# First-batch loads over 128 and 96 partitions, masks by matmul, partial products kept in open PSUM banks

## The chip, the cores and the metric

The kernel runs on one core of a Trainium2 chip. The metric is the device time of one execution in microseconds (us). A core has five engines with a queue of their own: TensorE (PE; its weight loads are listed apart as PEld), VectorE (DVE), ScalarE (ACT), GpSimd (POOL) and SyncE (SP), which here issues every DMA. A difference of about 0.3% (1.6 us) is what a measurement of this kernel can tell from no change.

## What is computed

Banded attention over 8 batches, 8 heads, 576 positions and 64 features a head, and then a gated block on its output:

```python
scores = scale * np.matmul(q, k.transpose(0, 1, 3, 2))
mask_plain = (rel >= 0) & (rel < 32)                          # heads 0 to 3
mask_dil = (rel >= 0) & (rel < 128) & (rel % 4 == 0)          # heads 4 to 7
attn = softmax(np.where(mask, scores, -1e9))
x = (attn @ v), heads joined                                  # (8, 576, 512)
h = np.maximum(x @ w_in, 0.0)                                 # w_in: 512 x 1024
u, v = h[..., :512], h[..., 512:]
v_n = (v - mean(v)) / np.sqrt(var(v) + 1e-06)
v_s = np.einsum('ts,bsd->btd', w_spatial, v_n) + b_spatial[None, :, None]
out = (u * v_s) @ w_out                                       # w_out: 512 x 512
```

The two weights `w_in` and `w_out` come as float64.

## The kernel before

**Tiling.** A pair of heads fills 128 partitions. For a pair, `heads_in` loads the keys and the queries (both transposed) into one of 12 buffers `kqv`, and `values_in` loads the values into another: four DMAs of 64 partitions, each row cut into nine runs of 64 numbers (L451). `unit` takes three blocks of 64 queries of two pairs: 24 score products of 32 queries by 64 keys (L469) that go to two PSUM banks, the mask added by DVE on the way out (L489), the maximum (L491), exponentials on ACT (one by one with their sums, L497, or all at once, L506, with the sum on DVE, L508), the division on POOL (L512), three transposes (L517) and a copy (L520). `weighted` multiplies by the values (L545): 36 products a call, two calls for two pairs, each with 64 rows of keys, and four that stand in a row use four different quarters of the array. `evacuated` and `features_in` turn the result into a rounded part `xh` and a remainder `xl`, four times for the 512 features.

**Precision.** Every large product is three products of rounded halves (hi by hi, hi by lo, lo by hi). For the weights `weight` makes the halves from the two words of a float64: a scaling on ACT (L319), four instructions on DVE (L321, L323, L326, L329), the rounding on ACT (L356), and the remainder by three matmuls and a copy (L335 to L339), by DVE (L280, L350) or by POOL. `weight_in` loads a block of 128 rows as two DMAs of 64 partitions (L297), since the two heads of a pair that stand together in `x` do not stand together in `w_in`.

**The rest of a batch.** `v_tile` (L614, L628) makes the half `v` of the hidden layer and normalises it, `upper` (L690, batch 0 only) the half `u`, `gate` (L711 to L713) the product with `w_spatial`. From batch 1 on `u`, and in every batch the output, come from `piece`: a product of two by two blocks with seven products (named 11, 21, 1, 2, 3, 22, 4) in place of eight, each of six matmuls (L831), whose inputs are sums and differences that `differences` (POOL, L821) and `factor` (ACT, L794, and DVE, L280) make. Every product has a PSUM bank of its own; the first is copied out by ACT (L874), and seven additions on DVE (L872) per half `m` put the results together.

**Order.** `Timeline.run` writes the program: every function above is a strand that asks for an engine with a cost and for buffers by tag (`kqv`, `mm`, `bank`, ...), and the strand that could start first, with a rank added, is recorded next. The ranks come from tables in the code. So each engine has one fixed order, and an engine waits where its next instruction isn't ready. `warm` fills gaps that the planner sees on PE before its time 30 with matmuls of zeros (L895); their number is fixed in the program.

Of the kernel before, what the change touches and what calls it, by code (L numbers as in the profile page):

```python
# [22 lines left out]
NEG = -(2.0**100)  # L23

# [123 lines left out]
def tile_banded_attention_gated_moe(  # L148
# [46 lines left out]
    BIG = NB * D  # L195

# [4 lines left out]
    def bufs(tag, shape, n, pool=const):  # L201
        return [pool.tile(shape, F32, name=f"{tag}{i}") for i in range(n)]


    tl = Timeline(
        dict(
            bank=bufs("bank", [P, 512], 8, ps),
            mm=[None] * 4,
            s=[None] * 2,
# [8 lines left out]
            ur=bufs("ur", [P, HS], 10),  # L218
            fac=[],
# [10 lines left out]
    kinds = tl.bufs["raw"][0][:, : 2 * KW].bitcast(BF16).rearrange("p (n k) -> p n k", n=4)  # L230
# [11 lines left out]
    for r in range(QB, P, QB):  # L242
        nc.vector.tensor_copy(kinds[r : r + QB], top)
    nc.vector.tensor_copy(masks, kinds[:, 0:1].broadcast_to([P, US + NS, KW]))

# [5 lines left out]
    for (far, g), n in cut.items():  # L251
        r = slice(g % 2 * 2 * QB, g % 2 * 2 * QB + 2 * QB)
        nc.vector.tensor_copy(masks[r, US * far + g // 2], kinds[r, n])
# [4 lines left out]
    nc.vector.tensor_scalar_mul(minus, draft, -1.0)  # L258
    ident = plus.bitcast(F32)
    halfneg = const.tile([P, 1], F32, name="halfneg")  # L260
    nc.gpsimd.memset(halfneg, -0.5)


    wi = [const.tile([P, NC, DFF], F32R, name=f"wi{n}") for n in "hl"]
    wo = [const.tile([P, NC, DM], F32R, name=f"wo{n}") for n in "hl"]
# [20 lines left out]

    staged = {}

    def weight_in(key, src):

        yield "kqv"
        (staged[key],) = yield DMA, 1.95, 1.5
        dtype = src[0].dtype
        place = staged[key][1][:, : 512 if dtype == F32 else 1024]
        rows = P // len(src)
        for i, part in enumerate(src):
            nc.sync.dma_start(place[i * rows : i * rows + rows].bitcast(dtype), part)  # L297
        tl.done("in", *key)

    def weight(key, hi, lo, dtype, how):  # L300

        yield [("in", *key)]
# [56 lines left out]
    def spatial_in(sc):  # L359
        yield "kqv"  # L360
        (staged[sc],) = yield DMA, 1.1, 1.5
        nc.sync.dma_start(staged[sc][1][:, :S], w_spT[:, sc, :])
        tl.done("in", sc)

    def spatial(sc):
# [6 lines left out]
        if sc < 4:  # L372
            nc.scalar.copy(wt[0][:, sc, :], w)
            if not (sc in (1, 2,)):
                yield DVE2, 0.75
                sub(wt[1][:, sc, :], w, wt[0][:, sc, :])
            for ts in (slice(0, HS), slice(HS, S)) if sc in (1, 2,) else ():
# [45 lines left out]
    def heads_in(b, hp, lo=0, hi=NU):  # L423
# [5 lines left out]
        got = yield DMA, 0.74 * (hi - lo), 1.5  # L429
# [25 lines left out]
    def unit(b, G, u):  # L455
# [3 lines left out]
        yield [("qk", b, hp, u) for hp in pairs] + ([("v", 0, 1)] if b == 1 else [])  # L459
        yield "s bank bank p"  # L460
        *held, pb = yield PE, 0.52, 0.0
# [698 lines left out]
```

## Time and profile before

| | |
|---|---|
| median of 3 runs | 548.06 us (546.82 to 548.44) |
| the profiled execution, first to last instruction | 544.7 us |
| median less that span | 3.4 us |
| PE, DVE, ACT, POOL busy | 98%, 80%, 56%, 39% |
| matmuls recorded | 7591 |

The page gives no other time of the profiled execution than its span; the 3.4 us are what a run takes beyond the first and the last instruction, as far as these two numbers tell. A plain f32 matmul (L335, L469, L545) has two records and the matmuls of zeros (L895) one, so counts of records and of instructions differ: 1152 score products in the program have 2304 records. Durations of matmuls overlap; the distance from one start to the next is what a matmul costs PE.

### The profile page before, as it was taken

The page shows a single profiled execution, that of the slowest core. Times are in us where ns is not written, and L with a number is a line of the kernel's source. Part 1 is how long each engine was busy: PE and PEld are TensorE (multiplying, and loading weights), DVE is VectorE, ACT ScalarE, POOL GpSimd, SP SyncE. Part 2 cuts the span into 40 slices and gives each one's busy share as a digit, 9 for nine tenths or more (in the row PEclk, how much of TensorE's full clock was granted, in tenths as well). Part 3 has the DMA queues.
Part 4 walks back from the last instruction along what each step waited for, and adds up shares of the span by engine and source line. Part 5 has one row for each costly group of instructions (what it writes and reads, how often), then busy time and mean ns, then how long its engine had stood idle before and what let it go on. Part 6 is the DMA issues. An engine that isn't in the chain of part 4 may idle for free.

```text
span 544.7 us, 18357 instructions
## 1 busy us (share of the span) xinstructions
PE 536.1 (98%) x7591; PEld 487.9 (90%) x7591; DVE 435.7 (80%) x1036; ACT 307.1 (56%) x939; POOL 215.1 (39%) x255
## 2 busy tenths in 40 slices
PE   9998999999999999999999999999999999999997
PEld 7766789999998899988999999988999899989997
DVE  5988778989956998489957998489956899479836
ACT  4787796455755555565454555556464565454312
POOL 3420385373426153524417163433417153253230
PEclk9999999999999999999999999999999999999999
DMA  8999741201463144511464135421454134301002
GB/s 236 250 185 339 162 105 59 91 22 66 109 160 91 45 134 90 150 52 55 113 127 132 45 113 106 122 75 56 113 121 147 44 113 94 65 12 44 34 1 87
DMA packets 97446, 56.65 MB, mean 104 GB/s; under 512 B 78290, under 2 KB 87506, under 8 KB 97364
## 3 DMA queue, kind: packets, MB, share of 16 engines
q1 hardware_dynamic: 97364, 55.50, 38.4%
q8 instruction: 59, 0.97, 0.8%
q14 instruction: 23, 0.19, 0.1%
HBM read 46.04 MB, written 9.44 MB: 102 GB/s over the span
## 4 chain that ended last, share of the span: by engine, by line
PE 93%; DMA 3%; ACT 2%; issue 1%; SPq 1%; DVE 0%; POOL 0%
PE bank L831 31%; PE bank L711 19%; PE bank L614 16%; PE bank L545 6%; PE bank L469 5%; PE bank L517 3%; PE bank L628 2%; PE bank L690 2%; PE bank L895 2%; PE bank L713 2%; PE bank L712 2%; PE bank L335 1%; DMA kqv<-in_vw_dram 1%; DMA kqv<-in_w_in_dram 1%; ACT p L497 1%
## 5 line engine op out<-in xcount | busy, mean ns | idle before, releaser
L872 DVE TENSOR_TENSOR ur<-ur,bank 128x288 f32<-128x288 f32 x210 | 87.4, 446 | 28.3 <-PE bank L831 27.9
L794 ACT CAST fac<-ur 128x288 fp32r<-128x288 f32 x112 | 46.0, 430 | 79.8 <-DVE ur L718 40.3
L711 PE MATMUL bank<-wth,vnh 128*128 128x288 f32 x256 | 76.5, 299 | 0.0
L280 DVE TENSOR_TENSOR fac<-ur,fac 128x288 fp32r<-128x288 f32 x112 | 60.5, 550 | 19.5 <-ACT fac L794 19.2
L711 PE MATMUL bank<-wth,vnl 128*128 128x288 f32 x256 | 75.6, 295 | 0.1
L711 PE MATMUL bank<-wtl,vnh 128*128 128x288 f32 x256 | 75.6, 295 | 0.0
L821 POOL TENSOR_TENSOR ur<-ur,ur 128x288 f32<-128x288 f32 x64 | 55.5, 877 | 44.1 <-DVE ur L718 34.0
L512 POOL TENSOR_TENSOR p<-p,rv 128x384 f32<-128x384 f32 x48 | 40.8, 851 | 74.5 <-DVE rv L510 63.4
L497 ACT ACTIVATE p<-p,nm 128x64 f32<-128x64 f32 x192 | 64.5, 337 | 8.8 <-DVE nm L491 8.7
L650 POOL TENSOR_TENSOR rs<-rs,halfneg 128x1 f32<-128x1 f32 (+1 forms) x40 | 29.3, 732 | 91.1 <-DVE rs L648 91.0
L831 PE MATMUL bank<-fac,woh 128*128 128x288 f32 x256 | 53.3, 298 | 0.1
L614 PE MATMUL bank<-wih,xl 128*128 128x512 f32 x128 | 50.1, 392 | 1.8 <-issue 1.8
L821 POOL TENSOR_TENSOR raw<-raw,raw 128x288 f32<-128x288 f32 x42 | 43.3, 1037 | 19.4 <-DVE fac L280 18.6
L614 PE MATMUL bank<-wih,xh 128*128 128x512 f32 x128 | 50.4, 394 | 0.0
L614 PE MATMUL bank<-wil,xh 128*128 128x512 f32 x128 | 50.2, 392 | 0.0
L711 PEld LDWEIGHTS bank<-wth,vnh 128*128 128x128 f32 x256 | 48.2, 188 | 0.4
L711 PEld LDWEIGHTS bank<-wth,vnl 128*128 128x128 f32 x256 | 48.1, 188 | 0.3 <-issue 0.3
L711 PEld LDWEIGHTS bank<-wtl,vnh 128*128 128x128 f32 x256 | 48.2, 188 | 0.0
L831 PEld LDWEIGHTS bank<-fac,woh 128*128 128x128 f32 x256 | 42.2, 189 | 2.4 <-ACT raw L572 0.4
L831 PE MATMUL bank<-fac,o 128*128 128x288 f32 x288 | 44.1, 297 | 0.0
L718 DVE SCALAR_TENSOR_TENSOR ur<-ur,bank 128x288 f32<-128x288 f32 x64 | 27.8, 447 | 19.7 <-PE bank L713 19.2
L831 PEld LDWEIGHTS bank<-fac,o 128*128 128x128 f32 x288 | 40.6, 188 | 1.6
(155 smaller groups left out, 1364.5 us busy)
## 6 DMA issues: line engine op xcount, KB each, us to landing
kqv<-in_vw_dram SPq DMA_DIRECT2D x128, 144.0 KB, 3.8
out_dram<-ur SPq DMA_DIRECT2D x64, 144.0 KB, 1.8
kqv<-in_kT_dram SPq DMA_DIRECT2D x30, 304.0 KB, 4.3
kqv<-in_qT_dram SPq DMA_DIRECT2D x30, 288.0 KB, 3.8
kqv<-in_w_in_dram SPq DMA_DIRECT2D x16, 256.0 KB, 5.5
kqv<-in_w_out_dram SPq DMA_DIRECT2D x4, 512.0 KB, 8.4
kqv<-in_w_spT_dram SPq DMA_DIRECT2D x5, 288.0 KB, 6.7
kqv<-in_kT_dram SPq DMA_DIRECT2D x2, 192.0 KB, 5.1
```

The source lines that it names most:

```text
L280: nc.vector.tensor_sub(out, a, b.bitcast(F32))
L497: nc.scalar.activation(p[:, e, j], p[:, e, j], AF.Exp, bias=nm[:, i : i + 1], accum_out=sm[:, i : i + 1])
L512: nc.gpsimd.tensor_mul(flat, flat, rv.unsqueeze(2).broadcast_to([P, 2 * US, KW]))
L545: nc.tensor.matmul(acc[j][1][1][i * D : i * D + D, (g - h * HB) * QB : (g - h * HB + 1) * QB], v[r, g, :], probs[b, G, u][1][r, e, q * QB ...
L614: nc.tensor.matmul(pm, x[c][a][:, cols], wi[w][:, c, NF:], start=c == 0 and n == 0, stop=c == NC - 1 and n == 2)
L650: nc.gpsimd.tensor_tensor(rs[:m], rs[:m], halfneg[:m], op=ALU.pow)
L711: nc.tensor.matmul(pv, vn[c][a][:, fs], wt[w][:, c, ts], start=n == 0, stop=False)
L718: nc.vector.scalar_tensor_tensor(ur, ur, 0.0, pv, op0=ALU.max, op1=ALU.mult)
L794: nc.scalar.copy(dst[:, 0, i, :], src)
L821: nc.gpsimd.tensor_sub(at(*to), at(*a), at(*c))
L831: nc.tensor.matmul(bank[:, :HS], left(i, w)[:, m * P : m * P + P], right, start=n == 0, stop=n == 5)
L872: op(ob[1], mine[src][1], bank[:, :HS])
```

## The change

- **Loads of the first batch.** A pair's two heads swap places for every second pair, so that a block of `w_in` is 128 rows in a row and takes one DMA. The values of batch 0 are loaded as they lie, 96 partitions by 1152 numbers, one DMA in place of four. From batch 1 on the four DMAs stay.
- **Attention of batch 0.** With 96 keys on the partitions, probabilities are laid out with a gap of zeros, six transposes of 96 columns take the place of three (each unit), two copies that of one, and the products with the values have 96 rows. Six matmuls of a spread identity with a mask (L776 of the changed kernel) open each unit's two banks, and the scores add to them, so that DVE no longer adds masks in batch 0; it takes two half maxima and, in five units of six, subtracts them.
- **Weights.** The two instructions that put the sign in place (L321, L323) become one shift; ACT's scaling is a Prelu. Eleven of the twelve remainders were made by PE or DVE, nine of them by PE; now seven are. Of the blocks of `w_spatial`, one in place of two goes by PE.
- **Open banks.** In `piece`, products 11, 2, 3 and 4 add to one bank, and 1 and 22 to another; ACT copies the running sum out between two products, and three additions on DVE remain of seven. A product that goes on in an open bank waits for the copy of the one before.
- **Room.** Batch 0's probabilities lie where the halves of `w_out` lie later, so `w_out`'s blocks wait until the first attention is done.
- **Order.** The rank tables, the order of the loads and the costs of DMAs in the planner are new.

```diff
...
+LOADS = """
+kq0b wi10 kq1b kq0a kq1a wi00 kq2 wi12 bias v0 kq3 wi03 v1 wo1 sp4 wi13 wo2 wi11 wi02 v3 v2 sp3 sp1 sp0 wi01
+sp2 wo3 wo0
+""".split()
...
+WAYS = {'wi1': 'GPDD', 'wi0': 'PPDP', 'wo': 'PPDP', 'sp': 'DDPD'}
+
+ALONG = {0: '010000', 1: '110110'}
...
+            ch=[None] * 4,
...
+            p0=[early[n][:, at : at + US * WIDE] for n, at in ((0, 1536), (1, 768), (1, 1248))],
+            pT0=[early[n][:, at : at + 2 * US * P] for n, at in ((0, 0), (0, 768), (1, 0))],
...
+    def masks_in():
+        yield DVE, 0.7
+        for r in range(QB, P, QB):
+            nc.vector.tensor_copy(kinds[r : r + QB], top)
+        yield DVE, 0.4
+        nc.vector.tensor_copy(masks, kinds[:, 0:1].broadcast_to([P, US + NS, KW]))
+        yield DVE, 0.15 * len(cut), 0.08
+        for (far, g), n in cut.items():
+            r = slice(g % 2 * 2 * QB, g % 2 * 2 * QB + 2 * QB)
+            nc.vector.tensor_copy(masks[r, US * far + g // 2], kinds[r, n])
+        tl.done("masks")
...
-        (staged[key],) = yield DMA, 1.95, 1.5
-        dtype = src[0].dtype
-        place = staged[key][1][:, : 512 if dtype == F32 else 1024]
-        rows = P // len(src)
-        for i, part in enumerate(src):
-            nc.sync.dma_start(place[i * rows : i * rows + rows].bitcast(dtype), part)
+        (staged[key],) = yield DMA, 1.4, 1.5
+        place = staged[key][1][:, : 512 if src.dtype == F32 else 1024].bitcast(src.dtype)
+        nc.sync.dma_start(place, src)
...
-        nc.scalar.activation(g, g, AF.Copy, scale=2.0**-112)
+        nc.scalar.activation(g, g, AF.Prelu, scale=2.0**-112, alpha=-(2.0**32))
         yield DVE2, 0.43
-        nc.vector.tensor_scalar(ti, gi, 3, 0x7FFFFFFF, op0=ALU.logical_shift_left, op1=ALU.bitwise_and)
-        yield DVE2, 0.68
-        nc.vector.scalar_tensor_tensor(gi, gi, 0x80000000, ti, op0=ALU.bitwise_and, op1=ALU.bitwise_or)
-        tl.add(-0.15 + key[-1] * 0.01, rounded(hi, g, ("hi", *key)))
+        nc.vector.tensor_scalar(gi, gi, 3, None, op0=ALU.logical_shift_left)
+        tl.add(RANKS[("rounded",)] + key[-1] * 0.01, rounded(hi, g, ("hi", *key)))
...
-        (big,) = yield DMA, 3.3, 1.5
-        src = vw[b, hp].rearrange("k (t j d) -> k t j d", j=2, d=D)
-        dst = big[1][:, :BIG].rearrange("p (t n d) -> p t n d", n=2, d=D)
-        for j in range(2):
-            for n in range(2):
-                nc.sync.dma_start(dst[j * D : j * D + D, :, n, :], src[n * QB : n * QB + KW, :, j, :])
+        if b == 0:
+            (big,) = yield DMA, 1.5, 1.5
+            nc.sync.dma_start(big[1][:ROWS, :BIG], vw[b, hp])
+        else:
+            (big,) = yield DMA, 3.3, 1.5
+            src = vw[b, hp].rearrange("k (t j d) -> k t j d", j=2, d=D)
+            dst = big[1][:, :BIG].rearrange("p (t n d) -> p t n d", n=2, d=D)
+            for j in range(2):
+                to = (j ^ hp % 2) * D
+                for n in range(2):
+                    nc.sync.dma_start(dst[to : to + D, :, n, :], src[n * QB : n * QB + KW, :, j, :])
...
+        *held, pb = yield PE, 0.52 if b else 0.98, 0.0
         s = [h[:, : US * KW].rearrange("p (e k) -> p e k", e=US) for _, h in held[1:]]
-        for e in range(US):
-            for q in range(4):
-                g = 2 * (US * u + e) + q // 2
-                kq = keys[b, pairs[q % 2]]
-                for j in range(2):
-                    r = slice(j * D, j * D + D)
-                    nc.tensor.matmul(
-                        s[j][q * QB : q * QB + QB, e, :],
-                        kq[r, WIN + S :].rearrange("p (u n i t) -> p u t n i", n=2, i=QB, t=US)[:, u, g // 2 % US, g % 2],
-                        kq[r, g * QB : g * QB + KW],
-                        start=True,
-                        stop=True,
-                    )
+        if b == 0:
+            for w, e in itertools.product(range(2), range(US)):
+                kind = cut.get((G >= NG // 2, 2 * (US * u + e) + w), 0)
+                nc.tensor.matmul(s[w][:, e, :], spread, kinds[:QB, kind], start=e == 0, stop=True, skip_group_check=e > 0)
+        for e, w, i, j in itertools.product(range(US), range(2), range(2), range(2)):
+            g = 2 * (US * u + e) + w
+            kq = keys[b, pairs[i]]
+            r = slice(j * D, j * D + D)
+            q, side = (2 * w + i, j ^ i) if b else (2 * i + j, w)
+            nc.tensor.matmul(
+                s[side][q * QB : q * QB + QB, e, :],
+                kq[r, WIN + S :].rearrange("p (u n i t) -> p u t n i", n=2, i=QB, t=US)[:, u, g // 2 % US, g % 2],
+                kq[r, g * QB : g * QB + KW],
+                start=b > 0,
+                stop=True,
+                skip_group_check=b == 0,
+            )
...
+        if b == 0:
+            yield DVE, 0.8 if along else 1.06, 0.08
+            tops = row(nm)
+            for w in range(2):
+                nc.vector.tensor_reduce(tops[:, :, w], s[w], axis=AX.X, op=ALU.max, negate=True)
+            if along:
+                nc.vector.tensor_scalar_mul(nm, nm, SCALE)
+            else:
+                for w in range(2):
+                    nc.vector.tensor_tensor(p[:, :, w], s[w], tops[:, :, w].unsqueeze(2).broadcast_to([P, US, KW]), op=ALU.add)
+                tl.give(*held)
...
+            yield "pt bank bank pT0"
+            *held, probs[n] = yield PE, 0.66
+            for e, w in itertools.product(range(US), range(2)):
+                at = e * WIDE + w * KW
+                nc.tensor.transpose(held[1 + w][1][:ROWS, e * P : e * P + P], pb[1][:, at : at + ROWS], ident)
+            tl.give(("p0", pb[1]))
+            for w in range(2):
+                yield ACT, 0.375, 0.105 * w
+                nc.scalar.copy(probs[n][1][:ROWS, w * US * P : (w + 1) * US * P], held[1 + w][1][:ROWS, : US * P])
...
+                pT = probs[b, G, u][1]
+                if b:
+                    r = slice((j ^ i) * D, (j ^ i) * D + D)
+                    left, right = v[r, t, n, :], pT[r, e, (2 * n + i) * QB : (2 * n + i + 1) * QB]
+                else:
+                    at = (n * US + e) * P + (2 * i + j) * QB
+                    left, right = v[:ROWS, t, j, :], pT[:ROWS, at : at + QB]
+                to = (g - h * HB) * QB
+                nc.tensor.matmul(acc[i][1][1][j * D : j * D + D, to : to + QB], left, right, start=True, stop=True)
...
+        if name != order[0]:
+            yield [("begun", b, kind, order[order.index(name) - 1])]
...
+        before = {"2": "11", "3": "2", "4": "3", "22": "1"}.get(name)
+        which = b, kind, m, name == "22"
+        if before:
+            yield [made(before)]
+        else:
+            yield "mm bank" if name == "21" else "ch bank"
         held = yield PE, 0.8
+        held = open_banks.pop(which) if before else held
         bank = held[1][1]
+        product(bank, b, kind, m, left, name, before is None)
         mine = parts.setdefault((b, kind, m), {})
+        of = {"21": "11", "1": "3", "22": "2"}.get(name)
+        if of:
+            yield [made(of)]
+            yield DVE, 0.372, 0.08
+            ob = mine[of]
+            nc.vector.tensor_add(ob[1], ob[1], bank[:, :HS])
+        else:
+            yield "ur"
+            (ob,) = yield ACT, 0.3, 0.1
+            mine[name] = ob
+            nc.scalar.copy(ob[1], bank[:, :HS])
+        tl.done(*made(name))
+        if name in ("21", "4", "22"):
+            tl.give(*held)
+        else:
+            open_banks[b, kind, m, name == "1"] = held
...```

On SP the first loads stand like this, from the load of a `w_spatial` block on. Names are buffer, source and size; x4 is four DMAs in a row. Before:

```order
L362 DMA kqv_80<-in_w_spT_dram 128x576
L451 DMA kqv_81<-in_vw_dram 64x9x64 x4
L297 DMA kqv_82<-in_w_in_dram 64x512 x2
L297 DMA kqv_83<-in_w_in_dram 64x512 x2
L297 DMA kqv_76<-in_w_in_dram 64x512 x2
L451 DMA kqv_74<-in_vw_dram 64x9x64 x4
```

and in the changed kernel, from the load of the bias on:

```order
L703 DMA kqv_80<-in_b_sp_dram 1x576 x2
L753 DMA kqv_81<-in_vw_dram 96x1152
L741 DMA kqv_82<-in_kT_dram 128x608
L742 DMA kqv_82<-in_qT_dram 128x576
L603 DMA kqv_83<-in_w_in_dram 128x512
L753 DMA kqv_84<-in_vw_dram 96x1152
L603 DMA kqv_85<-in_w_out_dram 128x512
```

Ten DMAs for two pairs' values and a `w_in` block have become three. On PE, the place ahead of the first products with the values (L545, in the changed kernel L903) had the last run of zeros (L895) and two remainders of weights:

```order
L895 MATMUL bank_64<-vnl_116 128x512 x12
L335 MATMUL bank_67<-kqv_82,plus 128x512
L336 MATMUL bank_67<-wih,minus 128x512
L337 MATMUL bank_67<-wil,plus 128x512
L335 MATMUL bank_68<-kqv_83,plus 128x512
L336 MATMUL bank_68<-wih,minus 128x512
L337 MATMUL bank_68<-wil,plus 128x512
L545 MATMUL bank_69<-pT_92,kqv_81 64x32
```

In the changed kernel the same remainder stands right behind the first half of these products, and a transposition of 96 rows (L860) follows:

```order
L903 MATMUL bank_69<-earlyh,kqv_81 64x32 x2
L903 MATMUL bank_70<-earlyh,kqv_84 64x32 x2
L640 MATMUL bank_67<-kqv_83,plus 128x512
L641 MATMUL bank_67<-wih,minus 128x512
L642 MATMUL bank_67<-wil,plus 128x512
L860 MATMUL bank_68<-plus,earlyh 96x128
L860 MATMUL bank_71<-plus,earlyh 96x128
```

The run of 12 zeros is gone there; in all 91 such matmuls have become 40 (18, 10, 8 and four single ones). The third place is PE at the end of the last batch, products 1 and 22 of the output for the halves m = 0 and 1. Before, four banks:

```order
L831 MATMUL bank_65<-fac_1371,o_888 128x288 x3
L831 MATMUL bank_65<-fac_1371,o_889 128x288 x3
L831 MATMUL bank_69<-fac_1371,o_888 128x288 x3
L831 MATMUL bank_69<-fac_1371,o_889 128x288 x3
L831 MATMUL bank_66<-fac_1372,o_888 128x288 x3
L831 MATMUL bank_66<-fac_1372,o_889 128x288 x3
L831 MATMUL bank_67<-fac_1372,o_888 128x288 x3
L831 MATMUL bank_67<-fac_1372,o_889 128x288 x3
```

and in the changed kernel two, each taken up again after the other's six matmuls:

```order
L1187 MATMUL bank_72<-fac_1358,o_899 128x288 x3
L1187 MATMUL bank_72<-fac_1358,o_900 128x288 x3
L1187 MATMUL bank_66<-fac_1358,o_899 128x288 x3
L1187 MATMUL bank_66<-fac_1358,o_900 128x288 x3
L1187 MATMUL bank_72<-fac_1337,o_899 128x288 x3
L1187 MATMUL bank_72<-fac_1337,o_900 128x288 x3
L1187 MATMUL bank_66<-fac_1337,o_899 128x288 x3
L1187 MATMUL bank_66<-fac_1337,o_900 128x288 x3
```

Between the two uses of bank 72 lie one other product of six matmuls and ACT's copy of the bank. Over the whole program 120 of the 210 products take up an open bank; in 6 of them one other product of six matmuls lies between, in 21 more what equals 8 to 12 matmuls of 288 columns, in the rest more. Runs of small tiled products (L469, L545) that stand between large ones are 52 where they were 58.

## Rows read from the trace of the kernel before

**Rows 1.** The page: engines' busy time; granted TensorE clock in 40 slices

```profile
PE 536.1 (98%) x7591; PEld 487.9 (90%) x7591; DVE 435.7 (80%) x1036; ACT 307.1 (56%) x939; POOL 215.1 (39%) x255
...
PEclk9999999999999999999999999999999999999999
```

**Rows 2.** Busy time by stretch: us, engines' busy us (instructions), PEclk, DMA share, GB/s

```profile
0.00:62.00 62.00, 58.33 (x801) 42.90 (x801) 49.64 (x111) 44.15 (x117) 15.67 (x29) 1.00 1.00 253
7.00:54.40 47.40, 44.77 (x679) 33.25 (x678) 40.49 (x83) 38.25 (x106) 9.90 (x10) 1.00 1.02 265
62.00:520.00 458.00, 456.39 (x6654) 424.15 (x6636) 372.00 (x892) 257.49 (x810) 192.73 (x219) 1.00 0.32 87
```

**Rows 3.** Groups by line: count, busy us, mean ns, idle before

```profile
L831 PE MATMUL bank<-fac,woh 128*128 128x288 f32 x256 | 53.3, 298 | 0.1
...
L895 PE MATMUL bank<-vnl 128*128 128x512 f32 x91 | 25.1, 424 | 1.0 <-DVE vnl L225 1.0
...
L872 DVE TENSOR_TENSOR ur<-ur,bank 128x288 f32<-128x288 f32 x210 | 87.4, 446 | 28.3 <-PE bank L831 27.9
L874 ACT COPY ur<-bank 128x288 f32<-128x288 f32 x30 | 11.9, 397 | 10.5 <-PE bank L831 9.8
```

**Rows 4.** SP's issues in order of time: start, us, DMAs

```profile
2.58 2.46 SPq L297 DMA_DIRECT2D kqv<-in_w_in_dram  x4
...
13.16 3.99 SPq L451 DMA_DIRECT2D kqv<-in_vw_dram  x4
...
28.77 0.54 SPq L297 DMA_DIRECT2D kqv<-in_w_out_dram  x1
29.40 10.69 SPq L451 DMA_DIRECT2D kqv<-in_vw_dram  x8
```

**Rows 5.** PE in order of time, the first 37 us: start, us, records

```profile
1.04 5.04 PE L895 MATMUL bank<-vnl 128*128 128x512 f32 x13 [1.04 <-DVE vnl L225]
6.01 0.76 PE L469 MATMUL bank<-kqv 64*32 64x64 f32 x48
6.70 6.18 PE L895 MATMUL bank<-vnl 128*128 128x512 f32 x26
...
15.90 1.27 PE L469 MATMUL bank<-kqv 64*32 64x64 f32 x96
...
31.64 1.06 PE L335 MATMUL bank<-kqv,plus 128*128 128x512 f32 x2
...
34.46 2.30 PE L545 MATMUL bank<-pT,kqv 64*64 64x32 f32 x144
36.70 0.87 PE L517 MATMUL bank<-plus,p 128*128 128x128 f32 x6
```

**Rows 6.** The chain that ended last, 49 to 53 us: start, us

```profile
49.36 1.83 issue
...
51.59 0.49 PE bank L381 x2
52.08 0.14 PE bank L382
```

**Rows 7.** DVE's groups in the first 56 us: count, busy us, mean ns

```profile
L323 DVE SCALAR_TENSOR_TENSOR kqv<-kqv,mid 128x512 uint32<-128x512 uint32 x11 | 8.7, 788 | 0.4
...
L491 DVE TENSOR_REDUCE nm<-p 128x6 f32<-128x384 f32 x6 | 3.3, 553 | 0.2
...
L508 DVE TENSOR_REDUCE sm<-p 128x6 f32<-128x384 f32 x2 | 1.1, 542 | 0.0
```

**Rows 8.** The chain in the last batch: start, us

```profile
528.82 1.59 PE bank L711 x12
...
530.70 0.02 issue
530.73 0.47 DVE ur L718
...
541.51 0.45 DVE ur L872
```

More of the change, by code (lines that the diff above doesn't have):

```diff
@@ new lines @@
+LOADS = """
+kq0b wi10 kq1b kq0a kq1a wi00 kq2 wi12 bias v0 kq3 wi03 v1 wo1 sp4 wi13 wo2 wi11 wi02 v3 v2 sp3 sp1 sp0 wi01
+sp2 wo3 wo0
+""".split()
+RANKS = {
+    ('bias',): 3.2,
+    ('fac', 'spare'): 0.82,
+    ('masks',): 0.35,
+    ('o', 'spare'): -0.17,
+    ('o', 'sums'): 0.0,
+    ('rounded',): 0.53,
+    ('sp', 0): 0.54,
+    ('sp', 1): 3.46,
+    ('sp', 2): 2.19,
+    ('sp', 3): 1.73,
+    ('sp', 4): 0.67,
+    ('u', 'spare'): 0.3,
+    ('u', 'sums'): 0.89,
+    ('wi', 0, 0): -3.26,
+    ('wi', 0, 1): -3.03,
+    ('wi', 0, 2): -2.15,
+    ('wi', 0, 3): -1.79,
+    ('wi', 1, 0): -2.09,
+    ('wi', 1, 1): -1.25,
+    ('wi', 1, 2): -1.13,
+    ('wi', 1, 3): 0.27,
+    ('wo', 0): -2.52,
+    ('wo', 1): -0.63,
+    ('wo', 2): -1.35,
+    ('wo', 3): 0.53,
+}
@@ L202, in bufs @@
         return [pool.tile(shape, F32, name=f"{tag}{i}") for i in range(n)]
+    early = [const.tile([P, NC, DM], F32, name=f"early{n}", tag=f"wo{n}").rearrange("p c d -> p (c d)") for n in "hl"]
+    WIDE = 2 * KW + QB
     tl = Timeline(
@@ L261, in tile_banded_attention_gated_moe, with room_made @@
     nc.gpsimd.memset(halfneg, -0.5)
+    nc.scalar.activation(work.tile([P, 1], F32, tag="rs", name="first", bufs=4), zeros[:, :1].bitcast(F32), AF.Exp)
     wi = [const.tile([P, NC, DFF], F32R, name=f"wi{n}") for n in "hl"]
-    wo = [const.tile([P, NC, DM], F32R, name=f"wo{n}") for n in "hl"]
+    wo = []
+    def room_made():
+        yield [("weighted", 0, G, h) for G in range(NG) for h in range(2)] + [("masks",)]
+        wo.extend(const.tile([P, NC, DM], F32R, name=f"wo{n}", tag=f"wo{n}") for n in "hl")
+        tl.done("room")
     wt = [const.tile([P, 4, S], F32R, name=f"wt{n}") for n in "hl"]
@@ L831, in product @@
             nc.tensor.matmul(
-                bank[:, :HS], left(i, w)[:, m * P : m * P + P], right, start=n == 0, stop=n == 5
+                bank[:, :HS], left(i, w)[:, m * P : m * P + P], right, start=fresh and n == 0, stop=n == 5, skip_group_check=not fresh
             )
@@ L889, in warm @@
+        r, h = {"21": (0, 0), "1": (1, 1), "22": (0, 1), "4": (1, 0)}.get(name, (None, None))
+        if r is None:
+            return
+        if kind == "u":
+            raw[b, h, 2 * r + m] = ob
+            tl.done("u", b, h, 2 * r + m)
+            return
+        now = tl.now
+        nc.sync.dma_start(out[b, (2 * r + m) * P : (2 * r + m) * P + P, h * HS : h * HS + HS], ob[1])
+        tl.now += 2.5
+        tl.give(ob)
+        tl.now = now
     def warm():
@@ L902, in tile_banded_attention_gated_moe @@
     tl.add(0.5, warm())
-    ways = ((POOL, PE, DVE, PE), (PE, PE, PE, PE), (PE, PE, DVE, PE))
-    halves = {}
+    who = {"P": PE, "D": DVE, "G": POOL}
+    loads = {}
     for half in (1, 0):
@@ L908, in tile_banded_attention_gated_moe @@
         for c in range(NC):
-            heads = [c // 2 * 4 + c % 2 + n for n in (0, 2)]
-            src = tuple(w_in[h * D : h * D + D, half] for h in heads)
-            halves[half, c] = weight_in(("wi", half, c), src)
-            r = (-1.72, -1.46, -1.5, -1.39)[c] if half else (-2.53, -2.81, -2.56, -2.84)[c]
-            tl.add(r, weight(("wi", half, c), wi[0][:, c, cols], wi[1][:, c, cols], w_in.dtype, ways[1 - half][c]))
-    outs = [weight_in(("wo", c), (w_out[c * P : c * P + P, 0],)) for c in range(NC)]
@@ L1029, in tile_banded_attention_gated_moe @@
+    for n, name in enumerate(LOADS):
+        tl.add(2 * n - 200, loads[name])
     turns = {}
@@ L1034, in put @@
         key = strand.__name__, turn
-        rank += shift.get(key, 0.0) + second.get(key, 0.0) * (b == 1) if b else first.get(key, 0.0)
+        rank += SHIFT.get(key, 0.0) + SECOND.get(key, 0.0) * (b == 1) if b else FIRST.get(key, 0.0)
         tl.add(rank, strand)
```

570 lines of the change are left out of this document (353 added, 217 removed).

## The prediction

> **What bounds the kernel now.** First the page's busy times and the stretches [rows 1, 2]. PE is busy 98% of the span, and from 62 to 520 us 456.4 of 458: whatever DVE or ACT win there is worth nothing unless PE gets less to do. Before 62 us the picture is another: PE looks busy (58.3 of 62), but the groups by line show 91 matmuls of zeros among it, 25.1 us [rows 3], and 3.7 us are plain waits. So some 29 of the first 62 us do nothing for the result, and 33 do. The DMA share says why: 1.00 from 0 to 62 us and 0.32 later, with DVE busy 40.5 of the 47.4 us between 7 and 54.4 [rows 2]. SP's issues name the worst piece: 16 DMAs of values; the four from 13.16 us kept the queue for 3.99 us and the last eight from 29.40 us for 10.69, where a block of `w_out` over 128 partitions took 0.54 [rows 4]. Until those values were there, the second half of the attention could not begin, and the chain has PE waiting 1.83 us at 49.36 for features of it [rows 6]. The change can win at the start, then, and almost nowhere else; the question is how much of the 29 us comes off and what new PE work is put in.
>
> **The change part by part.**
>
> *Zeros.* 91 become 40, which is in the program. The first 13 took 5.04 us, 0.39 each, the next 26 took 6.18, 0.24 each [rows 5]. The first run is now 18: 5.04 + 5 x 0.24 = 6.2; the other 22 take 5.3. 25.1 - 11.5 = 13.6 us come off, if real work or nothing at all stands there.
>
> *New work on PE, in batch 0.* Masks: 36 small matmuls that the trace does not show. From below, a score product of the same 64 columns, 0.76/24 = 0.03 us; from above a transposition, 0.87/6 = 0.145 [rows 5]: 1.1 to 5.2 us. I take 3.0, the middle, as they have the columns of the one and the full width of the other. Transposes: 18 more at 0.13 (between 0.87/6 and that less the overlap of its last): 2.4. Products with the values: the old ones took 2.30 us for two calls, 1.15 each [rows 5], and four in a row used four different quarters of the array. With 96 rows, only the two column halves alternate (the loop over j), so I double: 4 x 1.15 = +4.6. Ends: 0, if something else paces them, and one at a time, four times as long, +13.8. Sum +10.0.
> [...]
>
> *Work taken from PE.* Two remainders of weights fewer: two sets of L335 to L337 run from 31.64 to the next start at 34.46 [rows 5], 1.4 us each, -2.8. One block of `w_spatial` fewer: two times 0.63 us [rows 6], -1.3. Six runs of small products fewer: two runs of 48 records cost 2 x 0.76, one of 96 costs 1.27 [rows 5], 0.25 for each, -1.5. Sum -5.6.
>
> *Loads.* 16 value DMAs become four, 16 of `w_in` eight. SP spent 3.99 + 10.69 us on 12 value DMAs and some 0.6 on each of `w_in` (2.46/4); at 0.54 [rows 4] the 24 fewer save SP about 20 us of the first 45. I count no time for that itself: it decides only whether the attention can start earlier. What is late next is DVE and PE.
>
> *DVE up to the features of the last two pairs.* It was busy 40.5 us between 7 and 54.4 [rows 2], where the last of the four `xl` was made. Off: L323 for ten blocks, 10 x 0.79 = 7.9 [rows 7], and one block fewer stands ahead of that point, some 1.6. On: two more remainders by DVE at 1.4; half maxima and subtractions for the masks, sums in five units instead of two: some 2.0 (12 halves at about 0.3, 10 subtractions at 0.34 and three sums at 0.542 against six full maxima at 0.553 and 12 mask additions at 0.34; the maxima and sums are measured [rows 7], the 0.34 is assumed on both sides alike). So about 36 us of work from 7 us on: 43 at the earliest, 48 with the 7 us of waits and gaps that the old stretch had, cut by a third. Before it was 54.4.
>
> *PE up to the same point.* From the program: scores, masks, transposes, four calls with the values at 2.3, five remainders and half of `v_tile` are about 31 us; with zeros of 11.5 and the first us idle, 44. DVE and PE thus meet within a few us, and neither has slack. The waits of the first stage were 3.7 us; with half as many zeros to cover for lateness I take 4.7, +1.0. Ends: 1 us, if the loads are early (-2.7), and 12.
>
> *Open banks.* DVE loses 120 additions of 0.446, 53.5 us; ACT gains 90 copies of 0.397, 36 us [rows 3]. From 62 us on neither is what PE waits for (1.6 us idle in 458), so I count nothing. The added wait: a product waits for ACT's copy of the one before in its bank. That takes, from the start of the last matmul's successor, about 0.17 (its tail: one lasts 0.298 [rows 3], and the next starts 1.59/12 = 0.133 after it [rows 8]) + 0.02 + 0.40 + 0.02 = 0.61 us, with the hand-over as at 530.70 [rows 8] and the copy of L874 [rows 3]. The order has at least six matmuls, 6 x 0.133 = 0.8 us, between, and mostly over 1.6. Behind a waiting PE stands everything. It costs nothing as long as ACT is less than 0.2 us late in 6 places and 0.5 to 1 in 21 more.
>
> *ACT's Prelu, the shift, the room for `w_out`.* One instruction for one on ACT, and fewer on DVE: no time on PE. `w_out` waits for the attention of batch 0, but its first use is behind the first `gate`, beyond 90 us: nothing, unless the splits then crowd DVE.
>
> *The end.* Last matmul, a copy or an addition of about 0.4 and a DMA: as before (541.51 [rows 8] to 544.7). Nothing.
>
> Sum against the profiled span: 544.7 - 13.6 + 10.0 - 5.6 + 1.0 = 536.5 us. The median of the runs is 3.4 above that span, so 539.9; I say 540.0.
>
> **The rivals.**
>
> *Zeros turn into waits.* If the features of the last pairs come no earlier than 54 us, for instance since DVE stands behind late loads or POOL, every zero taken out is a wait: 544.7 + 10.0 - 5.6 + 3.4 = 552.5, slower. Place: PE ahead of the second half of `v_tile`. It decides from 9 us of added waits on. For it: DVE and PE have no slack there. Against: SP and DVE both lose work. 0.09.
>
> *ACT late for open banks.* 27 places with little cover, a cast of 0.4 us in ACT's way at each: 27 x 0.4 = 10.8 us, 551. For it: ACT's order is fixed and it waits for DVE and POOL often. Against: ACT is busy 56% [rows 1]. 0.06.
>
> *The clock.* The granted clock is 1.00 in every stretch [rows 1, 2], with PE filled by zeros where it had nothing else. [...] If 10 us of the early work ran at the 0.39 of the first zeros in place of 0.24 [rows 5], it would cost 6 us: 546. 0.06.
> [...]
>
> *Half the gain.* The loads come early but the units, one after the other through five engines, do not: waits of 7 to 10 us more than now less some zeros; 544 to 547. 0.11.
>
> *More.* Products with 96 rows cost what they did, masks 1 us, waits fall to 1: 540 - 4.6 - 2 - 3.7 = 530. 0.14.
>
> **How the numbers follow.** The forecast has 0.54 (534 to 544). Its own bounds, masks 1.1 to 5.2, values up to a few us more, waits 1 to 8, make 533 to 547. The range takes in "more" down to 531 and "half" and the clock up to 548, and leaves out the slower cases and a little below: 531 to 548. Faster by over 0.3%, below 546.4: the forecast, "more", two thirds of "half" and half the clock, some 0.79. Slower, over 549.7: the first two rivals less a part, 0.12. Within 0.3%, which is about what a measurement can tell from no change: 0.09.
>
> **What would show it.** In the changed kernel: zeros some 11 us; PE's waits before the first `gate` below 6 us; the four 96-row calls at about 2.3 us each; the last `xl` of batch 0 between 43 and 49 us; the first `gate` some 8 us earlier than before; PE still over 99% busy from 60 us on, and no wait of a piece's matmul for ACT's copy above 1 us in sum. The forecast is wrong if PE waits over 12 us before 60 us, if the 96-row products run one at a time, or if the distance from batch to batch grows.

## The result, and the profile after

The changed kernel takes 540.0 us (median of 4 runs, 539.74 to 540.77) against 548.25 (546.82 to 548.72): a ratio of 0.9848, 95% interval 0.9829 to 0.9867, or 8.3 us less. The forecast was 540.0, range 531 to 548, faster. The profiled execution took 540.14 us and its span is 538.3, so 1.8 us lie around it.

The page of the changed kernel, busy times, granted TensorE clock and DMA share in 40 slices [for before: rows 1]:

```profile
PE 530.5 (99%) x7580; PEld 487.7 (91%) x7580; DVE 392.4 (73%) x924; ACT 330.0 (61%) x996; POOL 209.8 (39%) x253
...
PEclk9979999999999999999999999999999999999999
DMA  8958550302453144331463125511463126201002
```

Busy time by stretch of the changed kernel, columns as in [rows 2]:

```profile
0.00:62.00 62.00, 58.56 (x892) 45.63 (x893) 49.49 (x127) 40.95 (x89) 15.41 (x29) 0.92 0.81 252
24.50:34.70 10.20, 9.45 (x121) 7.46 (x123) 4.80 (x17) 4.05 (x9) 2.59 (x3) 0.50 0.73 219
62.00:514.00 452.00, 451.96 (x6571) 422.84 (x6551) 332.79 (x775) 281.10 (x887) 188.66 (x218) 1.00 0.32 87
```

From 62 us on PE is full, and DVE's load fell from 372.0 us in 458 to 332.8 in 452. New is the third slice of the clock: from 24.5 to 34.7 us it was granted at half (0.50). Before it was at 1.00 in every stretch [rows 2]. PE in order of time around it, in the changed kernel (start, us, records; in brackets the wait ahead):

```profile
21.27 0.89 PE L782 MATMUL bank<-kqv 64*32 64x64 f32 x48
22.09 0.50 PE L1261 MATMUL bank<-vnl 128*128 128x512 f32 x1
22.53 0.49 PE L776 MATMUL bank<-earlyl 32*128 32x64 bf16 x6
22.95 0.42 PE L782 MATMUL bank<-kqv 64*32 64x64 f32 x11
25.25 1.28 PE L782 MATMUL bank<-kqv 64*32 64x64 f32 x37 [1.88 <-issue]
26.46 4.05 PE L903 MATMUL bank<-earlyh,kqv 96*64 96x32 f32 x72
30.45 2.08 PE L640 MATMUL bank<-kqv,plus 128*128 128x512 f32 x2
...
37.84 1.06 PE L640 MATMUL bank<-kqv,plus 128*128 128x512 f32 x2
...
39.96 2.99 PE L903 MATMUL bank<-earlyh,kqv 96*64 96x32 f32 x96
```

PE stops in the middle of a group of score products for 1.88 us, and behind it 72 records of products of 96 rows take 4.0 us, where 96 later ones take 2.8 to the next start; the first two matmuls of a remainder (L640) take 2.08 against 1.06. The page calls the wait "issue": PE waited for nothing that the profile shows. PE's waits in the whole changed kernel, with the engine or DMA waited for:

```profile
PE bank L782 <- issue: 1.9, 1, 1.9
PE bank L1261 <- DVE vnl L517: 1.0, 1, 1.0
PE bank L1187 <- ACT fac L1150: 0.7, 1, 0.7
PE bank L782 <- DMA kqv<-in_qT_dram: 0.5, 2, 0.3
PE bank L1187 <- DVE fac L577: 0.4, 1, 0.4
```

No piece waits for an ACT copy. SP's issues of values and of the two last blocks of `w_in` ahead of them, in the changed kernel [before: rows 4]; the 16 DMAs of values of batch 0 kept the queue for 18.2 us before (four of them, from 22.47 us on, for 3.50), the four here for 2.7:

```profile
10.04 0.32 SPq L753 DMA_DIRECT2D kqv<-in_vw_dram  x1
...
12.59 0.33 SPq L753 DMA_DIRECT2D kqv<-in_vw_dram  x1
...
17.33 6.84 SPq L603 DMA_DIRECT2D kqv<-in_w_in_dram  x2
26.44 2.06 SPq L753 DMA_DIRECT2D kqv<-in_vw_dram  x2
```

Where PE's time went, worked out from both traces as the distance from each matmul's start to the next, summed by kind; a wait ahead of a start is counted apart. The third column is the forecast's term, the last is the kernel with four more zeros (below), in which the clock stays up:

| PE, us | before | changed | forecast | measured | four more zeros |
|---|---|---|---|---|---|
| zeros | 24.1 | 11.6 | -13.6 | -12.5 | 13.4 |
| masks (L776) | 0 | 1.8 | +3.0 | +1.8 | 1.6 |
| transposes | 15.9 | 18.9 | +2.4 | +3.0 | 18.3 |
| products with the values | 36.2 | 42.1 | +4.6 | +5.9 | 40.3 |
| remainders, `w_in` and `w_out` | 12.7 | 11.2 | -2.8 | -1.5 | 10.0 |
| remainders, `w_spatial` | 2.6 | 1.2 | -1.3 | -1.3 | 1.2 |
| scores | 32.2 | 33.1 | 0 | +0.9 | 32.2 |
| pieces, `v_tile`, `upper`, `gate` | 412.0 | 410.2 | -1.5 | -1.8 | 410.2 |
| waits between them | 4.3 | 3.5 | +1.0 | -0.8 | 3.3 |
| sum | | | -8.2 | -6.4 | |

The start of the last matmul moved from 541.18 to 534.78 us, which is the 6.4. Changed against the last column, the small rows (masks, transposes, values, remainders, scores) hold 4.7 us more: that is what half the clock cost.

### The profile page after: what moved, and what is told of

The parts are those of the page before. It is cut to its first block, busy times and chain, and to the rows that moved or that the text cites. A ratio compares the mean times of both kernels' runs of the same rounds, so it can differ in the third digit from the quotient of the medians.

```text
span 538.3 us, 18217 instructions
## 1 busy us (share of the span) xinstructions
PE 530.5 (99%) x7580; PEld 487.7 (91%) x7580; DVE 392.4 (73%) x924; ACT 330.0 (61%) x996; POOL 209.8 (39%) x253
## 2 busy tenths in 40 slices
DMA  8958550302453144331463125511463126201002
## 4 chain that ended last, share of the span: by engine, by line
PE 94%; DMA 3%; issue 1%; POOL 1%; DVE 0%; ACT 0%; SPq 0%; POOLq 0%
PE bank L1187 32%; PE bank L1064 19%; PE bank L967 16%; PE bank L903 8%; PE bank L782 6%; PE bank L870 3%; PE bank L981 3%; PE bank L1043 2%; DMA kqv<-in_qT_dram 2%; PE bank L1066 2%; PE bank L1065 2%; PE bank L640 1%; DMA kqv<-in_w_in_dram 1%; PE bank L860 1%; POOL ur L1177 1%
## 5 line engine op out<-in xcount | busy, mean ns | idle before, releaser
L1236 ACT COPY ur<-bank 128x288 f32<-128x288 f32 x120 | 46.7, 396 | 51.2 <-PE bank L1187 50.0
L1150 ACT CAST fac<-ur 128x288 fp32r<-128x288 f32 x112 | 46.6, 434 | 44.8 <-DVE ur L1071 24.4
L577 DVE TENSOR_TENSOR fac<-ur,fac 128x288 fp32r<-128x288 f32 x112 | 55.8, 513 | 24.4 <-ACT fac L1150 20.5
L831 ACT ACTIVATE p<-p,nm 128x64 f32<-128x64 f32 x168 | 56.4, 338 | 2.8 <-DVE nm L825 2.8
L1187 PE MATMUL bank<-fac,woh 128*128 128x288 f32 x256 | 53.0, 298 | 0.0
L1231 DVE TENSOR_TENSOR ur<-ur,bank 128x288 f32<-128x288 f32 x90 | 38.8, 443 | 14.9 <-PE bank L1187 13.5
L1177 POOL TENSOR_TENSOR raw<-raw,raw 128x288 f32<-128x288 f32 x42 | 39.9, 957 | 23.3 <-DVE fac L577 18.6
L854 POOL TENSOR_TENSOR p<-p,rv 128x384 f32<-128x384 f32 x42 | 35.2, 847 | 32.6 <-ACT p L831 16.1
L1187 PE MATMUL bank<-fac,o 128*128 128x288 f32 x288 | 44.7, 297 | 1.1 <-ACT fac L1150 0.7
L1187 PEld LDWEIGHTS bank<-fac,o 128*128 128x128 f32 x288 | 41.4, 188 | 3.9 <-ACT fac L1150 0.9
```

Of the source, the lines that this page charges most:

```text
L577: nc.vector.tensor_sub(out, a, b.bitcast(F32))
L831: nc.scalar.activation(p[:, e, j], p[:, e, j] if b else s[j][:, e], AF.Exp, bias=nm[:, i : i + 1], scale=1.0 if b else SCALE, accum_out=sm ...
L854: nc.gpsimd.tensor_mul(flat, flat, spread_out(rv))
L1150: nc.scalar.copy(dst[:, 0, i, :], src)
L1177: nc.gpsimd.tensor_sub(at(*to), at(*a), at(*c))
L1187: nc.tensor.matmul(bank[:, :HS], left(i, w)[:, m * P : m * P + P], right, start=fresh and n == 0, stop=n == 5, skip_group_check=not fresh)
```

## The experiments

**Are the zeros the gain by themselves?** The kernel before, with every second zero left out:

```diff
+        turn = 0
         while tl.now < 30:
-            nc.tensor.matmul(...)
+            turn += 1
+            for _ in range(turn % 2):
+                nc.tensor.matmul(...)
...
```

> The kernel before with every second of its 91 matmuls of zeros left out, 45 in all, nothing else touched. Theory: the zeros come off only because the loads and the attention behind them come earlier; without that, what they filled becomes waiting, and the time stays at 545 to 549 us (548.25 before). Rival: the zeros themselves were the cost, and leaving them out alone gives 45 x 0.25 = 11 us, about 537. Where the clock falls for want of work, it ends above 549.

548.4 us, ratio to before 0.9999 (0.9973 to 1.0025): the theory. The zeros went from 24.1 to 15.5 us, and all of it came back. PE's waits in the first 62 us of this kernel:

```profile
PE bank L517 <- POOL p L512: 4.6, 1, 4.6
PE bank L545 <- issue: 4.1, 2, 3.3
PE bank L469 <- issue: 2.1, 1, 2.1
```

The granted clock of those 62 us fell to 0.92 as well. In this profile, of a run of 549.4 us, the waits grew by 7.7 us, and the same small products took 4.7 us more, as parts of them ran at half the clock. So in the old order the zeros covered something else that was late, and kept the clock up; they could come off only together with what they covered. The waits name POOL's probabilities and PE's own instructions (the last section), and no load.

**What was late: the loads.** The changed kernel with the blocks of `w_in` and `w_out` loaded in halves again:

```diff
-        nc.sync.dma_start(place, src)
+        for i in range(2):
+            nc.sync.dma_start(place[i * 64 : i * 64 + 64], src[i * 64 : i * 64 + 64])
```

> The changed kernel with each block of w_in and w_out loaded by two DMAs of 64 partitions in place of one of 128. Theory: PE waits for loads only up to 18 us, the rows that hold it there are those of queries and keys, and SP has room: 12 more issues of some 0.5 us move those loads by 2 us at most; 540 to 542. Rival: the wide loads are what brings the attention forward, and without them 4 to 8 us of waits come back, 544 to 548.

546.4 us (544.1 to 548.4), 0.9953 (0.9932 to 0.9974) of before: the rival. Some 6 of the 8.3 us gained are gone by this edit alone, and not by the clock: it was at half for 10.2 us here too, while PE's waits grew by 6.0 us. What the wide loads alone would bring to the old order, no run tells. PE's waits in its first 62 us:

```profile
PE bank L783 <- DMA kqv<-in_qT_dram: 4.2, 3, 3.2
PE bank L783 <- issue: 2.9, 1, 2.9
```

The packets of the first 24 us, this kernel's first, the changed kernel's second:

```profile
DMA packets 2603, 5.47 MB, mean 228 GB/s; under 512 B 348, under 2 KB 1372, under 8 KB 2602
...
q1 hardware_dynamic: 2602, 5.45, 93.4%
```

```profile
DMA packets 3045, 7.11 MB, mean 296 GB/s; under 512 B 339, under 2 KB 1363, under 8 KB 3043
...
q1 hardware_dynamic: 3043, 7.08, 92.4%
```

The DMA engines are as busy with the halves, 93% against 92%, and move 23% less. The queries of the last pair land at 23.35 us in place of 17.99. SP loses too: its issues run without a break from 0.73 to 7.25 us, and these queries are issued at 15.45 us in place of 10.98. How much is the narrower transfer and how much the additional issues, this run does not split.

**Which zeros are needed?** The changed kernel with its first 18 zeros alone (`range(int(turn <= 18))`):

> The changed kernel with its first 18 matmuls of zeros alone; the 22 that stand later, 5.9 us in all, are left out. Theory: up to 18 us the kernel waits for queries and keys that are being loaded, so 18 of the 22 fill waiting time and the other four bring 1.4 us: 538.5 to 540.5 if the clock stays as it is. Rival one, PE is the bound from the start: all 5.9 us come off, 534. [...]

539.0 us (538.35 to 541.02), 0.9839 (0.9804 to 0.9874), not to be told from the changed kernel: the theory. In its profile, of the run of 541.0 us, the 22 zeros, 5.9 us, turned into 3.6 us of waits for queries (0.5 before) and 1.0 us for ACT and POOL; the half clock came at 10.7 to 14.1 and 27.8 to 34.6 us, as long in all as before. Until 18 us the changed kernel waits for loads, and zeros there cost nothing.

**What brought the clock down?** Eight more zeros at 22.1 us, ahead of the wait:

```diff
...
+            for _ in range(9 if turn == 39 else 1):
...
```

> The changed kernel with eight more matmuls of zeros at 22.1 us, 1.8 us in all, in front of the wait of 1.88 us that PE had at 23.37 us and that was followed by half the clock from 24.5 to 34.7 us. Theory: the wait is one for instructions that are still on their way, the zeros fill it, the clock stays up, and the 4.5 us that the half clock cost come off: 534 to 536.5, with a granted clock of 1.00. Rival one: the wait comes all the same, as it hangs on the number of instructions, and the clock falls as before: 541 to 542. Rival two: the clock falls for another reason than the wait, without a wait at 23 us: 539 to 541.

536.9 us (536.37 to 537.92), 0.9796 (0.9766 to 0.9826), granted clock 0.999 or 1.0 in each run, the wait gone. The theory, though 0.4 us above its numbers, as another wait grew: for queries, 1.6 us in place of 0.5.

```profile
PE bank L782 <- DMA kqv<-in_qT_dram: 1.6, 1, 1.6
```

Then four more in place of eight:

> The changed kernel with four more zeros (0.9 us) where the run with eight more had them, at 22.1 us. Theory: half the wait is filled, the rest of about 1 us is too short to bring the clock down, and the time is that of the run with eight, 536.9, or up to 0.9 us less: 536 to 537. Rival: what is left of the wait is enough, and the clock falls: 539 to 541.

536.0 us (535.41 to 537.0), 0.9755 (0.9734 to 0.9776), clock 0.999 or 1.0 in each run: the theory. The same stretch as in the changed kernel, here, and PE's waits up to 62 us:

```profile
24.50:34.70 10.20, 9.02 (x210) 7.53 (x209) 7.79 (x24) 7.58 (x17) 2.59 (x3) 1.00 1.00 301
```

```profile
PE bank L782 <- issue: 1.2, 1, 1.2
PE bank L1264 <- DVE vnl L517: 1.0, 1, 1.0
PE bank L782 <- DMA kqv<-in_qT_dram: 1.0, 2, 0.6
```

Neither this wait of 1.2 us nor one of 1.5 in the later set of this kernel brought the clock down; the clock fell in the one of 1.88. In the first 40 us of all 14 traces, half the clock came with or behind each of the ten waits of 1.7 to 4.6 us, whether for instructions, queries or probabilities. Length alone is not it: in the kernel before, 1.83 us at 49.36 us [rows 6], among large products, brought no fall. Nor do these runs split the shorter wait from the busier stretch ahead of it, as the zeros change both. Four zeros, 0.9 us of nothing, return 4.7 us of clock, and the time falls by 4.0 us in this set and 2.9 in the later one. (The zeros of this profile rose by 1.8 us, not 0.9: the full clock was granted from 5.8 us on, in the changed kernel's from 4.0, so the first ones took longer.)

**Two products of 96 rows in a row.** First all products of one half of the columns, then the other:

```diff
-            for g, i, j in itertools.product(blocks, range(2), range(2)):
+            spots = list(itertools.product(blocks, range(2), range(2)))
+            for g, i, j in spots if b else sorted(spots, key=lambda s: s[2]):
```

> The changed kernel with the 288 products of 96 rows in another order: first all of one half of the columns, then all of the other, in place of one and the other by turns. Theory: two products that stand in a row run beside each other only where they use different halves; by turns one took 0.030 us, so without turns each takes 0.06: 288 x 0.03 = 8.6 us more, 548 to 550. Rival: something else paces them (the rows that stream or the weight loads), and the time stays at 540 to 541.

553.0 us (551.23 to 558.14), 1.0103 (1.0044 to 1.0162): the theory, and more than its number. Products in this kernel at half the clock and at full, and its first 62 us (the profile is of the run of 558.1 us):

```profile
26.33 7.49 PE L904 MATMUL bank<-earlyh,kqv 96*64 96x32 f32 x72
...
48.35 1.82 PE L904 MATMUL bank<-earlyh,kqv 96*64 96x32 f32 x28
```

```profile
0.00:62.00 62.00, 58.69 (x705) 48.72 (x706) 35.55 (x96) 29.70 (x67) 12.40 (x25) 0.75 0.60 187
```

With the tail of 0.17 us off, a record, of which a product has two, costs 0.059 us at full clock (1.65/28), where by turns it costs 0.030 (8.76/288 in the kernel with four more zeros). At half the clock it is 0.10 here. The medians lie 13.0 us apart, and the 4.4 beyond 8.6 go with the clock: its mean over a run was 0.969 to 0.984, where the changed kernel had 0.989 to 0.994. In the profile it was at 0.75 in the first 62 us, and part of that (41.5 to 48.3 us) began with no wait of PE right ahead of it.

**Open banks.** All 120 products that go on in an open bank closed, and DVE adding in place of 90 of ACT's copies (the other 30 products end in an addition on DVE as it is, so DVE has 180 additions here, 30 fewer than before the change):

```diff
-        product(bank, b, kind, m, left, name, before is None)
+        product(bank, b, kind, m, left, name, True)
...
-            nc.scalar.copy(ob[1], bank[:, :HS])
+            if before:
+                nc.vector.tensor_add(ob[1], wo[0][:, 0, :HS].bitcast(F32), bank[:, :HS])
+            else:
+                nc.scalar.copy(ob[1], bank[:, :HS])
```

> The changed kernel with the products closed one by one: the 90 products that go on in an open bank start afresh, and in place of ACT's copy DVE adds the bank to other numbers (a block of weights, so the sums that leave the kernel are not the reference's). DVE gets 90 x 0.45 = 40 us more, ACT 36 us less. Theory: nothing in this stage waits for either, and the time stays at 539.5 to 541. Rival: DVE at four fifths busy lets the factors come late, and PE waits some us more: 542 to 548.

542.5 us (541.2 to 546.9): inconclusive, as the clock of its runs went from 0.984 to 0.997. The same edit on the kernel whose clock stays up:

> The kernel with four more zeros at 22.1 us, whose clock stays up, and in it the 90 products that go on in an open bank closed and added by DVE in place of ACT's copy (the sums that leave the kernel are not the reference's). Theory: this costs what the rows of the pieces rose by with the same edit before (1.1 us in their matmuls and 1.0 in their waits): 537.5 to 538.5 against 536.0. Rival: what was measured there came from the clock of the first stage, and the edit costs nothing: 535.8 to 536.5.

540.0 us (539.24 to 540.74), 0.9849 (0.9821 to 0.9877), clock 1.0 in each run: 4.0 us slower than without the edit, or 2.9 against the later set of that kernel, and more than the theory's number. PE's waits of the pieces in this kernel:

```profile
PE bank L1187 <- DVE fac L577: 0.9, 2, 0.4
PE bank L1187 <- ACT fac L1150: 0.7, 1, 0.7
PE bank L1187 <- DVE ur L1237: 0.4, 1, 0.4
PE bank L1187 <- DVE p L823: 0.2, 1, 0.2
```

The pieces rose by 1.3 us in their matmuls and 1.3 in their waits (2.4 for 1.1, with those too short for the list); what is left of the 3.6 us between the two profiles lies in the first stage, in waits for queries and in small differences of several kinds. In the new order the open banks are worth some 3 us. What they are worth against the old order, which was made for DVE's additions and had 1.6 us of idle PE from 62 us on, no run here tells.

**One load earlier.** The queries and keys of the last pair ahead of the first values, by the list of loads:

> The changed kernel with eight more zeros at 22.1 us, and with the queries and keys of the last pair loaded ahead of the values of the first pair (issued at 10.5 us, and waited for until 19.1 us; the values are not needed before 26 us). Theory: the wait of 1.6 us for these queries goes down by 0.5 to 1.6 us, and so does the time: 535.3 to 536.4. Rival: the DMA engines are full up to there whatever the order, and the next load is late instead: 536.5 to 537.5.

591.1 us. This tells nothing of the load: the planner made another order of all eight batches of it. The stretch of 62 us from 186 us on, for example:

```profile
186.00:248.00 62.00, 55.95 (x748) 52.31 (x748) 36.92 (x79) 32.60 (x95) 20.11 (x23) 0.92 0.34 92
```

PE waits there for probabilities from POOL and for factors, and the clock is at 0.92. The same move on SP alone, every other instruction in its place, on the kernel with four more zeros:

> The kernel with four more zeros at 22.1 us, and in it, on SP alone, the values of the first pair issued right behind the queries and keys of the last pair, where they stood right ahead of them; every other instruction keeps its place. Theory: these queries come 0.5 to 1.5 us earlier, the wait for them at 18 us (0.4 us in the profile of the kernel with four more zeros, up to 2.2 in others) goes, and what follows moves up: 535.0 to 535.8 against 536.0. Rival: PE then only comes earlier to the instructions that are not there yet, and waits longer for them: 535.8 to 536.5.

537.8 us (535.78 to 539.08), 0.9816 (0.9779 to 0.9853), above the numbers of both. The wait for queries is gone (the profiled span, 534.0, is the shortest of all), and the two runs above 538 had a clock of 0.997 and 0.994. With eight zeros, and beside it the kernel with four and the old order of loads:

> The kernel with the values of the first pair issued behind the queries and keys of the last pair, now with eight more zeros at 22.1 us in place of four. Theory: with four its runs had a granted clock of 0.994 to 0.999 over the whole, so what failed was the clock, since PE came to the missing instructions earlier; eight fill that wait, the clock stays at 0.999 or more in all runs, and the time is 535 to 536.3. Rival: the order of loads itself makes it slower or more uneven, and the time stays at 537 to 539.

> The kernel with four more zeros at 22.1 us and the loads as in the changed kernel, once more, on the same chip as the other of this call, as its measure. Theory: 535.5 to 537, a granted clock of 0.999 or more in each run. Rival: the even times of its first five runs were chance, and some runs fall to half the clock like the changed kernel: 536 to 540, with a clock below 0.997 in some.

536.6 us (535.94 to 537.34), 0.9776 (0.9752 to 0.9800), and 537.1 (536.56 to 537.93), 0.9787 (0.9763 to 0.9810); the clock was 0.999 or 1.0 in all nine runs. So it was the clock, as far as these numbers tell: no trace shows a run of that set in which it fell. What the earlier load gives beyond that, 0.6 us, is within the intervals. The kernel with four more zeros (536.0 and 537.1 in two sets) is faster than the kernel before and the changed one.

## Why the prediction was right, point by point

**The time, 540.0.** Right, and to the digit by luck. The sum gave a span of 536.5, it was 538.3; and the 3.4 us put around the span were 1.8, since the median of the runs of before had been set against one profile that was below it. The 1.8 us in the span are themselves two errors: the terms came out 2.9 us better than forecast, and the clock, which was not in the sum, cost 4.7. The mechanism was right: zeros come off together with earlier loads, new small products take a part of that back, and after 62 us little changes.

**Zeros, -13.6.** -12.5. What is left was forecast well (11.5, and 11.6 measured; the first 18 took 5.7 us for 6.2). It was taken from 25.1 us of busy time, in which the tail of each run counts; from start to start the old zeros took 24.1. "If real work or nothing at all stands there" was the right condition: without the rest of the change it is waiting, as half the zeros left out of before showed.

**New work, +10.0.** Without the half clock (last column of the table) +8.1: masks 1.6 in place of 3.0 (0.045 us each, nearer to the lower bound's row, a score product, than to a transposition), transposes 18.3 - 15.9 = +2.4 as said, products with the values +4.1 for 4.6. That 96-row products run beside each other where they take the two halves of the columns by turns, as the forecast assumed, is shown by the run that put one half in a row: a record cost 0.059 us there, 0.030 by turns. No row of before has a product of 96 rows; the doubling to 2.3 us a call was the author's estimate, and the kernel with four more zeros has 2.19 (8.76/4).

**Work taken, -5.6.** Without the half clock -2.7 and -1.3 for the remainders, as said; the pieces and what stands among them 1.8 less, for 1.5 from fewer switches. Part of the 1.8 may be the open banks' doing: closed, these rows took 1.3 more in the new order. The runs don't split it.

**Loads, "I count no time for that itself".** The step that was undersized as a reason, though the sum holds it under the zeros: the loads are not one condition among several, in the new order they carry some 6 of the 8.3 us. What is late in the first 18 us of the changed kernel is neither DVE nor PE but queries and keys behind full DMA engines (the queue of the loads 89.7% busy in the first 18.1 us), and the forecast did not look there.

**The wait at 49.36 us** [rows 6] was read wrongly. The forecast put it down to late features. The row says "issue", and in the trace of before the features in question were there: `xl` by 49.15 us.

```profile
48.39 0.76 DVE L280 TENSOR_TENSOR xl<-raw,xh 128x576 fp32r<-128x576 f32 x1 [1.89 <-ACT xh L587]
```

A packet of 16 KB on the queue for instructions ended at 49.77 us, and PE went on at 51.19.

**DVE, 43 to 48 us for the last `xl`.** It ended at 50.9 us, a miss by 3. DVE was busy 35.4 of the 43.9 us from 7 us to there, so the 36 of work were right; the gaps were 8.5 us, more than the old 7, where the forecast had cut them to 5. The first `gate` came 4.7 us earlier (84.6 for 89.3), not 8.

**Waits, +1.0.** They fell by 0.8, to 3.5 us.

**The clock, a rival with 0.06 and 6 us.** It happened, and cost 4.7 us, beside and not in place of the forecast. The rows of before show no fall, 1.00 in every stretch [rows 1, 2]; the changed kernel had 0.50 for 10.2 us, behind one gap of 1.88 us between small products, and real work stood in the rest. Left out of the sum, it is its largest error. Slow zeros did stand in a row, the first 13 at 0.39 us each against 0.24 [rows 5]; the first record of the granted clock in that trace, at full, starts at 4.9 us.

**ACT late, 0.06.** It did not happen: no wait for a copy.

**Open banks, nothing.** Right against before as far as PE's idle time goes, wrong as a statement on the new order: closing them costs some 3 us there. "Neither is what PE waits for" held at DVE's load before, in an order made for it, and was carried over to another order.

## What to carry to other kernels

Filler work on TensorE stood here where something else was late (half of it left out alone: 548.4 us, ratio 0.9999); take it out only together with what it covers, and leave a little where PE would otherwise stand still among small products, since four matmuls of nothing here bought 4.7 us of clock, some 3 to 4 us of time. Load over all 128 partitions in one transfer where the layout allows it: engines as busy, 92% against 93%, moved 30% more bytes here (296 GB/s against 228). An experiment on a kernel that a planner orders must pin the order, or it measures the planner.

## What the runs showed of the hardware that was not expected

PE stood still for its own instructions, 1.88 us in the changed kernel and 1.83 before, as far as times can show it. The waits of PE that the profile calls "issue" end behind a packet of 16 KB of the instruction queue (59 such packets in the changed kernel, 0.97 MB, against 15,160 records of PE and PEld). From the packets and the starts in the traces:

| kernel | packet, us | PE goes on at | after the packet's end |
|---|---|---|---|
| before | 48.76 to 49.77 | 51.19 | 1.42 |
| changed | 22.75 to 23.76 | 25.25 | 1.49 |
| 18 zeros alone | 24.19 to 25.25 | 26.65 | 1.40 |
| halves of `w_in` | 30.44 to 31.71 | 33.12 | 1.41 |
| four more zeros | 23.45 to 24.47 | 25.88 | 1.41 |
| before, half the zeros | 20.29 to 21.54 | 22.87 | 1.33 |
| before, half the zeros | 36.91 to 38.33 | 39.92 | 1.59 |

The 14 traces have 22 such waits of over 0.2 us, and every one ends 1.26 to 1.65 us after such a packet. With eight more zeros the packet ended at 24.30 us, PE came to that group of products at 25.83, 1.5 us later, and there was no wait. Those of over 0.4 us fell among small score products, products with the values or transpositions, where a score product or a product with the values takes 0.016 to 0.03 us a record and instructions are used up fastest, and once (before) behind a stretch of large ones. Why the packet starts that late, whether for the loads that fill the DMA engines then or for another reason, was not tried.

Most of the 59 packets show no wait behind them, and where one did it cost 0.2 to 3.3 us.

In one trace the clock fell while PE had no wait at all: with products of one column half in a row it had been at full from 38.1 us, and was at half from 41.5 to 48.3 us, while PE was busy throughout.
